# Reordering the start-up of a fused gated-attention and state-space kernel: where three turns' TensorE blocks stand

## The chip, the core and the metric

The kernel runs on one core of a Trainium2 chip. The metric is the device time of one execution in microseconds (us); of several runs the median counts. The engines are named as in the profile: PE is TensorE (PEld its weight loads), DVE is VectorE, ACT is ScalarE, POOL is GpSimd, SP is SyncE, which here only issues DMAs.

## What is computed

Four batches of eight heads, 768 steps, 48 features per head. A gated linear recurrence is followed by a projection, a second recurrence with a gate, and a projection back (float32 throughout; the weights arrive as float64):

```python
for t in range(S):
    state = alpha[:, :, t, :, None] * state + np.einsum('bhd,bhe->bhde', k[:, :, t], v[:, :, t])
    y[:, :, t] = np.einsum('bhd,bhde->bhe', q[:, :, t], state)
# x: y with the heads side by side, (4, 768, 384)
proj = x @ w_in                       # 384 -> 2 * 512
val, gate = proj[..., :512], proj[..., 512:]
for t in range(S):
    h = a[0, 0] * h + val[:, t, :]
    ys[:, t, :] = h
silu = gate * (1.0 / (1.0 + np.exp(-gate)))
return silu * ys @ w_out              # 512 -> 384
```

## The kernel before

**Tiling.** The 768 steps of a batch are cut into three groups of 256 steps, so there are N = 12 groups, each of two chunks of 128 steps (c = 0, 1). The recurrence is done by chunk: cumulative products of alpha (two DVE scans, one forwards, `prod`, one backwards, `inv`) scale the queries and keys into `Z`; `scores` multiplies them, `masks` keeps the causal part in `A`, `values` multiplies `A` with v, `keys` turns the keys into `ktm`, `state` sums keys times values, `carried` adds what the earlier chunks left. `join` copies the result out of PSUM into `y_sb` and puts the heads side by side in `xT` with eight small DMAs and two copies. Then four `block(n, cc)`, one for each 128 of the 512 inner features: `project` (12 PE matmul instructions, values first, then gate), `hidden` (a DVE scan of 256 steps), `gate` (Silu on ACT, and a product on POOL into `f`). `output(n)` multiplies `f` with w_out: 16 matmul instructions for two chunks, evacuated by ACT and stored by SP.

**Stages.** Everything is written out in program order, and every engine works its own part of that order strictly in turn; semaphores between the engines come from the tiles. So the order of the source lines is the order of each queue: if PE reaches a matmul whose input is not there, all later matmuls wait. In turn n of the last loop the projections of group n run beside the attention of group m = n + 1, the DVE steps of group n + 2 (the generator `products`, advanced by `go(count)`, `count` yields at a time) and the loads of group n + 3 (`ahead`).

Groups 0 to 2 are loaded with steps on the partitions (`load_natural`) and are turned by PE transposes (`turned`, L605; for keys and queries followed by a DVE product, `natural_qk`, L620). From group 3 on a layout is loaded (`load_raw`, four DMAs for each of a, k, q) that DVE can transpose itself (L660). For those groups `products` yields seven times: after turning a (with `first`, L671), after the scan `prod` (L674), after the scan `inv` (L695), after turning k, multiplying it (L704), turning q, multiplying it. `check_alpha` is a pass of ACT over the raw alphas (L631).

**Buffers that matter here.** Raw buffers: two sets, group m in set m % 2. v: two. `f`: one. `xT`, `Z`: two. PSUM banks 0, 1 and 6 go round for `mm`; pairs of banks (4, 5) and (2, 3) alternate for `pair_of`. Scans `hidden` wait in DVE's queue behind whatever stands before them.

**Lines to follow.** L1002 is the ACT copy of the turned alphas of group 2 into `aT`; L827 the matmuls of a block; L835 its scan, L842 its Silu, L843 its POOL product; L856 output matmuls; L864 and L865 their evacuation and store; L717 keys; L727 scores; L742 and L743 the far masks on ACT and POOL; L754 the near masks on DVE; L786, L765, L776 state, values, carried; L795, L796, L802 and L812 the join. L543 to L560 turn float64 words of the weights into float32, in the shadow of group 0's blocks; the last of these products, for w_out, is done on POOL at 44.4 us. L430 is `load_raw`, L445 `load_natural`, L454 `load_v`.

The functions that the diff touches:

Of the kernel before, what the change touches and what calls it, by code (L numbers as in the profile page):

```python
# [13 lines left out]
AF = mybir.ActivationFunctionType  # L14
# [337 lines left out]
def fast(  # L352
# [21 lines left out]
    nc = tc.nc  # L374
# [3 lines left out]
    C = 128  # L378
    G = 2
# [27 lines left out]
    def pair_of(*dims, dtype=FP32, which=None):  # L407
        if next(next_pair) if which is None else which:
            return [end_ps.tile([C, *dims], dtype, tag=f"b{b}", name="pair") for b in (4, 5)]
        t = both()  # L410
        n = dims[0] * dims[1]
        return [t[:, i, 0:n].rearrange("p (x y) -> p x y", x=dims[0]).bitcast(dtype) for i in range(2)]

    def both():
        return ps.tile([C, 2, 4 * C], FP32, tag="b23", name="pair")
# [5 lines left out]
    def load_raw(name, m, engines):  # L421


        b, g = divmod(m, NG)
        src = {"a": alpha, "q": q, "k": k}[name]
        t = raw_bufs[m % NR][name]
        n = 0
        for i in range(2):
            for odd in range(2):
                engines[n % len(engines)].dma_start(  # L430
                    out=t[ds(64 * i + 32 * odd, 32), :, 0:NT * D - 32 * odd],
                    in_=src[b, i::2, ds(g * GC, GC), :]
                    .rearrange("h (c j) d -> c h (j d)", c=32)[:, :, 32 * odd:])
                n += 1
# [3 lines left out]
    def natural(name, m):  # L438
        flat = raw_bufs[m % NR][name].rearrange("p h n -> p (h n)")[:, 0:G * H * 64]
        return flat.rearrange("p (c h d) -> p c h d", c=G, h=H)  # L440
# [10 lines left out]
    def load_v(m, engine, cs=range(G)):  # L451
        b, g = divmod(m, NG)
        for c in cs:
            engine.dma_start(out=vs[m % NV][:, c, :, 0:D],  # L454
                             in_=v[b, :, ds(g * GC + c * C, C), :].rearrange("h p d -> p h d"))
# [34 lines left out]
    alphas = aT[:, 0:4 * GC].rearrange("p (h n) -> p h n", h=4)  # L490
# [111 lines left out]
    def turned(name, m, c, tp):  # L602

        for p in range(4):
            nc.tensor.transpose(tp[:, p, :], natural(name, m)[:, c, 2 * p:2 * p + 2, :], ident)  # L605
# [17 lines left out]
    def check_alpha(m):  # L623

        if m < NAT:
            src = natural("a", m)[:, :, :, 0:D]
        else:
            src = raw_bufs[m % NR]["a"].rearrange("p h (j d) -> p h j d", d=D)[:, :, :, 0:32]
        _, x, y, z = src.shape
        junk = p1.tile([C, x, y, z], BF16, tag="junk", name="junk")  # L630
        nc.scalar.activation(junk, src, AF.Relu, bias=minus, accum_out=above[:, m:m + 1])  # L631
# [159 lines left out]
    def join(m, engines, later=False):  # L791

        y = ys.pop(m)
        y_sb = p2.tile([C, 4, GC], FP32, tag="y_sb", name="y_sb")
        nc.scalar.activation(y_sb[:, 1::2], y[1], AF.Copy)  # L795
        nc.scalar.activation(y_sb[:, 2], y[0][:, 1], AF.Copy)  # L796
        xT = xTs[m] = p2.tile([C, NK, GC], FP32, tag="xT", name="xT")

        def in_place():
            for h in (0, 4):  # L800
                kk, row = divmod(h * D, C)
                nc.scalar.activation(xT[ds(row, D), kk], y[0][ds(16 * h, D), 0], AF.Copy)  # L802

        if not later:
            in_place()
        for h in (1, 5, 3, 7, 2, 6):
            s, a = divmod(h, 4)
            d = 0
            while d < D:
                kk, row = divmod(h * D + d, C)  # L810
                size = min(D - d, C - row)
                engines[s].dma_start(out=xT[ds(row, size), kk], in_=y_sb[ds(64 * s + d, size), a])  # L812
                d += size
        return in_place
# [25 lines left out]
    def gate(n, cc, pg):  # L840
        sg = p2.tile([C, GC], FP32, tag="sg", name="sg")
        nc.scalar.activation(sg, pg, AF.Silu)  # L842
        return lambda: nc.gpsimd.tensor_mul(fs[n][:, cc, :], sg, hhs.pop((n, cc)))  # L843

    def block(n, cc):
        pv, pg = project(n, cc)
        hidden(n, cc, pv)
        gate(n, cc, pg)()

    def output(n, banks=(None, None)):  # L850
        b, g = divmod(n, NG)
        os = [mm(DM, b=b) for b in banks]

        def part(ccs, c):
            for cc in ccs:
                nc.tensor.matmul(os[c], fs[n][:, cc, ds(c * C, C)], w_out[:, cc, :],  # L856
                                 start=(cc == 0), stop=(cc == NI - 1))

        def finish():
            for c in range(G):  # L860
                part(range(split, NI), c)
            for c in range(G):
                o_sb = p3.tile([C, DM], FP32, tag="o_sb", name="o_sb")
                nc.scalar.activation(o_sb, os[c], AF.Copy)  # L864
                nc.sync.dma_start(out=out[b, ds(g * GC + c * C, C), :], in_=o_sb)  # L865

        split = NI - 1 if n else NI // 2
        for c in range(G):
            part(range(split), c)
        return finish  # L870


    SP, ACT = nc.sync, nc.scalar
# [98 lines left out]
    banks = pair_of(4, C, dtype=U32)  # L972
# [18 lines left out]
    for cc in range(NI):  # L991
# [4 lines left out]
            low_word(cc + 3)  # L996
        words(cc + 2)
        times()
    finish = output(0)
    for c, tp in enumerate(pair_of(4, C)):  # L1000
        turned("a", 2, c, tp)
        nc.scalar.activation(alphas[:, :, ds(c * C, C)], tp, AF.Copy)  # L1002
    check_alpha(2)
    load_raw("k", 3, [SP])
    load_raw("q", 3, [SP])
    for _ in products(2):
# [5 lines left out]
    for n in range(1, N):  # L1012
        m = n + 1
        att = m < N
        steps = products(n + 2) if n + 2 < N else iter(())

        def go(count):
            for _ in range(count):
                next(steps, None)


        def ahead():
            if n + 3 < N:
                loads(n + 3)
            if n + 2 < N:
                load_v(n + 2, SP)

        if n < 3:
            if n == 1:
                block(n, 0)  # L1030
                for times in [natural_qk(m, name, c, tp) for c in range(G)
                              for name, tp in zip("kq", pair_of(4, C))]:
                    times()
                block(n, 1)
            ahead()
            for c in range(G):
                keys(m, c)
            for c in range(G):
                scores(m, c)
            go(1)  # L1040
            for c in range(G):
                masks(m, c)
            if n == 2:
                block(n, 0)
                go(1)
                block(n, 1)
                go(1)
            else:
                block(n, 2)
                go(1)  # L1050
            state(m, 0)
            values(m, 0)
            values(m, 1)
            state(m, 1)
            carried(m, 0)
            carried(m, 1)
            join(m, (nc.gpsimd, nc.gpsimd) if m == 2 else (SP, SP))
            if n == 2:
                go(2)
                block(n, 2)  # L1060
            go(1)
            block(n, 3)
            go(10)
            output(n)()
            continue

        if n == 3:
            for c in range(G):  # L1070
                scores(m, c, 1 - c)
                masks_apart(m, c)
            for c in range(G):
                keys(m, c)
            ahead()
            go(4)
        else:
            state(n, 0)
            values(n, 0)
            values(n, 1)  # L1080
            state(n, 1)
            carried(n, 0)
            carried(n, 1)
            in_place = join(n, (SP, nc.gpsimd), later=True)
            if att:
                scores(m, 0, 1)
                masks_apart(m, 0)
                in_place()
                scores(m, 1, sc=[mm(4, C, b=b) for b in "01"])
                masks_apart(m, 1)  # L1090
                keys(m, 0, "6")
                keys(m, 1, "4")
            else:
                in_place()
            next_mm = itertools.cycle("160")
            ahead()
            go(4)
            output(n - 1, "50")()
        for cc in range(NI):
            block(n, cc)  # L1100
            go(1)
            if cc == 0 and n == N - 1:
                next(end, None)
            if cc == 2 and n > 3:
                for _ in itertools.islice(checks, 2):
                    pass
        if n == N - 2:
            end = check_end()
            next(end)
# [61 lines left out]
```

## Time and profile before

| | us |
|---|---|
| median of 3 runs (lowest, highest) | 291.07 (291.03, 291.84) |
| the profiled execution | 291.08 |
| its span, first to last instruction | 289.3 |
| busy: PE, PEld | 279.4, 227.2 |
| busy: DVE, POOL, ACT | 211.2, 139.2, 109.1 |
| DMA moved | 42.08 MB, mean 145 GB/s |

The granted TensorE clock is 1.000 over the whole span. The first 30 us are start-up: loads, turning and attention of groups 0 and 1. Group 0's blocks run from 30.25 us, its output from 40.72, turn one (n = 1) from 47.18, turn two's scores start at 72.19, turn three's at 93.90, and from there each turn takes 21.5 to 21.9 us. A row of the timeline gives start, duration, engine, line, operation, tiles and count; in brackets stands the idle time of the engine before it and what ended it. [...] neighbouring matmuls overlap; the distance from start to start is the time that one takes.

### The profile page before, as it was taken

The page shows a single profiled execution, that of the slowest core. Times are in us where ns is not written, and L with a number is a line of the kernel's source. Part 1 is how long each engine was busy: PE and PEld are TensorE (multiplying, and loading weights), DVE is VectorE, ACT ScalarE, POOL GpSimd, SP SyncE. Part 2 cuts the span into 40 slices and gives each one's busy share as a digit, 9 for nine tenths or more (in the row PEclk, how much of TensorE's full clock was granted, in tenths as well). Part 3 has the DMA queues.
Part 4 walks back from the last instruction along what each step waited for, and adds up shares of the span by engine and source line. Part 5 has one row for each costly group of instructions (what it writes and reads, how often), then busy time and mean ns, then how long its engine had stood idle before and what let it go on. Part 6 is the DMA issues. An engine that isn't in the chain of part 4 may idle for free. (4 is left out here: it accounts for less than half of the span.)

```text
span 289.3 us, 6236 instructions
## 1 busy us (share of the span) xinstructions
PE 279.4 (97%) x2353; PEld 227.2 (79%) x2353; DVE 211.2 (73%) x263; ACT 109.1 (38%) x242; POOL 139.2 (48%) x165
## 2 busy tenths in 40 slices
PE   7699999999999999999999999999999999999985
PEld 6478877885886988788788788788788788687874
DVE  5998896999999999399599599599589580131221
ACT  2447634432441626316316415416416415313110
POOL 7147792375532765526725725625734734633130
PEclk9999999999999999999999999999999999999999
DMA  9999969999997992992991991991892400201101
GB/s 130 163 162 299 376 129 185 173 250 211 231 220 106 221 200 53 215 205 54 228 189 43 217 204 42 206 212 48 191 198 77 113 2 25 73 0 30 69 5 61
DMA packets 70734, 42.08 MB, mean 145 GB/s; under 512 B 47508, under 2 KB 69656, under 8 KB 70696
## 3 DMA queue, kind: packets, MB, share of 16 engines
q1 hardware_dynamic: 68240, 39.78, 69.8%
q0 software_dynamic: 1408, 1.62, 2.3%
q8 instruction: 20, 0.33, 0.5%
q10 hardware_dynamic: 1048, 0.20, 0.4%
q14 instruction: 18, 0.15, 0.2%
HBM read 33.33 MB, written 4.72 MB: 131 GB/s over the span
## 5 line engine op out<-in xcount | busy, mean ns | idle before, releaser
L827 PE MATMUL mm<-xT,w_in 128*128 128x256 f32 x576 | 127.7, 380 | 0.3 <-ACT A L742 0.3
L827 PEld LDWEIGHTS mm<-xT,w_in 128*128 128x128 f32 x576 | 108.7, 190 | 17.7 <-issue 0.6
L843 POOL TENSOR_TENSOR f<-sg,hh 128x256 f32<-128x256 f32 x48 | 40.4, 843 | 87.2 <-ACT sg L842 61.8
L835 DVE TENSOR_TENSOR_SCAN hh<-a_dec,hh,mm 128x256 f32<-128x256 f32 x32 | 23.7, 741 | 49.6 <-PE mm L827 44.9
L856 PE MATMUL mm<-w_out,f 128*128 128x384 f32 x176 | 59.4, 489 | 0.1
L842 ACT ACTIVATE sg<-mm 128x256 f32<-128x256 f32 x48 | 18.5, 385 | 98.7 <-PE mm L827 96.6
L750 POOL TENSOR_TENSOR A<-A,mask 128x512 f32<-128x512 f32 x32 | 47.7, 1519 | 5.5 <-ACT A L749 5.4
L856 PEld LDWEIGHTS mm<-w_out,f 128*128 128x128 f32 x176 | 32.5, 190 | 21.4 <-POOL f L843 1.0
L812 POOL DMA_DIRECT2D xT<-y_sb x44 | 22.7, 521 | 28.4 <-ACT y_sb L796 26.8
L674 DVE TENSOR_TENSOR_SCAN prod<-aT,first 128x1024 f32<-128x1024 f32 x10 | 23.4, 2340 | 0.3
L695 DVE TENSOR_TENSOR_SCAN inv<-aT,last 128x1025 f32<-128x1025 f32 x10 | 22.9, 2294 | 0.3
L765 PE MATMUL pair<-A,v 128*64 128x128 f32 x352 | 21.3, 274 | 0.0
L864 ACT ACTIVATE o_sb<-mm 128x384 f32<-128x384 f32 x22 | 10.8, 491 | 25.4 <-PE mm L856 25.2
L727 PE MATMUL pair<-Z 48*128 48x128 f32 x272 | 18.9, 282 | 0.8 <-DVE first L640 0.3
L727 PEld LDWEIGHTS pair<-Z 48*128 48x128 f32 x272 | 16.4, 187 | 3.7 <-issue 2.1
L765 PEld LDWEIGHTS pair<-A,v 128*64 128x64 f32 x352 | 19.1, 137 | 0.0
L743 POOL TENSOR_TENSOR A<-A,mask 128x512 f32<-128x512 f32 x8 | 10.1, 1274 | 17.9 <-ACT A L742 17.9
L660 DVE STREAM_TRANSPOSE Z<-raw_k 128x1024 f32<-128x1024 f32 x9 | 18.4, 2047 | 0.0
L660 DVE STREAM_TRANSPOSE aT<-raw_a 128x1024 f32<-128x1024 f32 x9 | 18.4, 2046 | 0.0
L660 DVE STREAM_TRANSPOSE Z<-raw_q 128x1024 f32<-128x1024 f32 x9 | 18.2, 2024 | 0.0
L835 DVE TENSOR_TENSOR_SCAN hh<-a_dec,mm 128x256 f32<-128x256 f32 x16 | 10.8, 676 | 8.6 <-PE mm L827 7.0
L786 PEld LDWEIGHTS st<-v,ktm 128*64 128x64 f32 x320 | 11.4, 137 | 3.5 <-issue 3.5
(128 smaller groups left out, 300.7 us busy)
## 6 DMA issues: line engine op xcount, KB each, us to landing
raw_k<-in_k_dram SPq DMA_DIRECT2D x24, 192.0 KB, 5.3
raw_q<-in_q_dram SPq DMA_DIRECT2D x24, 192.0 KB, 6.6
v<-in_v_dram SPq DMA_DIRECT2D x24, 192.0 KB, 7.1
raw_a<-in_alpha_dram SPq DMA_DIRECT2D x23, 192.0 KB, 4.0
out_dram<-o_sb SPq DMA_DIRECT2D x22, 192.0 KB, 4.0
raw_a<-in_alpha_dram SPq DMA_DIRECT2D x18, 176.0 KB, 4.5
raw_k<-in_k_dram SPq DMA_DIRECT2D x18, 176.0 KB, 5.5
raw_q<-in_q_dram SPq DMA_DIRECT2D x18, 176.0 KB, 7.0
```

What stands on the lines that cost most here:

```text
L660: nc.vector.transpose(out=to.rearrange("p h (c j) -> p h j c", j=NT), in_=raw_bufs[m % NR][name].rearrange("p h (j d) -> p h j d", d=D)[:, ...
L674: nc.vector.tensor_tensor_scan(out=prod, data0=al, data1=first.rearrange("p h n -> p (h n)"), initial=0.0, op0=ALU.mult, op1=ALU.max)
L695: nc.vector.tensor_tensor_scan(out=inv[:, ::-1], data0=aT[:, ::-1], data1=lasts[:, 0:4 * GC + 1][:, ::-1], initial=0.0, op0=ALU.mult, op1= ...
L727: nc.tensor.matmul(sc[i][:, p, :], Z[rows, p, 1, cols], Z[rows, p, 0, cols], start=True, stop=True)
L750: nc.gpsimd.tensor_mul(A[:, i], A[:, i], mask_all())
L765: nc.tensor.matmul(ys[m][i][ds(64 * s, 64), e, ds(c * C, C)], v_sb[:, c, 2 * p + i, :], A[:, i, p, :], start=(c == 0 and e == 0), stop=Fal ...
L812: engines[s].dma_start(out=xT[ds(row, size), kk], in_=y_sb[ds(64 * s + d, size), a])
L827: nc.tensor.matmul(pj, w_in[cc][vg][:, kk, :], xT[:, kk, :], start=(kk == 0), stop=(kk == NK - 1))
L835: nc.vector.tensor_tensor_scan(out=hh, data0=a_dec[:, cc:cc + 1].to_broadcast([C, GC]), data1=pv, initial=prev_h[cc][:, GC - 1:GC] if n % ...
L842: nc.scalar.activation(sg, pg, AF.Silu)
L843: return lambda: nc.gpsimd.tensor_mul(fs[n][:, cc, :], sg, hhs.pop((n, cc)))
L856: nc.tensor.matmul(os[c], fs[n][:, cc, ds(c * C, C)], w_out[:, cc, :], start=(cc == 0), stop=(cc == NI - 1))
```

## The change

Four edits, all of order:

- `output` takes a function `between`, called after chunk 0's first-half matmuls and before chunk 1's. For group 0 it turns group 2's alphas, copies them and checks them; before, this came after both chunks' first half.
- Turn one starts with the turning of group 2's keys and queries and has its blocks 0 and 1 together behind it; a step of `products` stands between the two. The next group's loads are split: alphas before group 2's keys, and keys, queries and v behind the join.
- Turn two starts with the loads and block 0, then keys and scores; its block 2 comes before the state and not after the join. Group 2's join issues half of its DMAs from SP and half from POOL, not all from POOL.
- Turn three takes two steps of `products` ahead of its blocks and not four, and what is left of them after its last block.

```diff
-    def output(n, banks=(None, None)):
+    def output(n, banks=(None, None), between=lambda: None):
...
         split = NI - 1 if n else NI // 2
-        for c in range(G):
-            part(range(split), c)
+        part(range(split), 0)
+        between()
+        part(range(split), 1)
         return finish
...
-    finish = output(0)
-    for c, tp in enumerate(pair_of(4, C)):
-        turned("a", 2, c, tp)
-        nc.scalar.activation(alphas[:, :, ds(c * C, C)], tp, AF.Copy)
-    check_alpha(2)
+
+    def alphas_2():
+        for c, tp in enumerate(pair_of(4, C)):
+            turned("a", 2, c, tp)
+            nc.scalar.activation(alphas[:, :, ds(c * C, C)], tp, AF.Copy)
+        check_alpha(2)
+
+    finish = output(0, between=alphas_2)
...
             if n == 1:
-                block(n, 0)
                 for times in [natural_qk(m, name, c, tp) for c in range(G)
                               for name, tp in zip("kq", pair_of(4, C))]:
                     times()
+                block(n, 0)
+                go(1)
                 block(n, 1)
-            ahead()
+                load_raw("a", n + 3, [SP])
+            else:
+                ahead()
+                block(n, 0)
             for c in range(G):
                 keys(m, c)
...
             if n == 2:
-                block(n, 0)
-                go(1)
                 block(n, 1)
                 go(1)
-            else:
-                block(n, 2)
-                go(1)
+            block(n, 2)
+            go(1)
             state(m, 0)
...
-            join(m, (nc.gpsimd, nc.gpsimd) if m == 2 else (SP, SP))
-            if n == 2:
-                go(2)
-                block(n, 2)
+            join(m, (SP, nc.gpsimd) if m == 2 else (SP, SP))
+            if n == 1:
+                for name in "kq":
+                    load_raw(name, n + 3, [SP])
+                load_v(n + 2, SP)
             go(1)
             block(n, 3)
...
             for c in range(G):
                 keys(m, c)
             ahead()
-            go(4)
+            go(2)
...
+        go(10)
         if n == N - 2:
```

## Prediction

> **What bounds the kernel now.** I read the page's busy shares first, then TensorE's timeline from end to end, then the waits of the one stretch in which it was not periodic, and last the landing times of the loads that this stretch uses.
>
> ```profile
> PE 279.4 (97%) x2353; PEld 227.2 (79%) x2353; DVE 211.2 (73%) x263; ACT 109.1 (38%) x242; POOL 139.2 (48%) x165
> ```
>
> TensorE is busy 97% of the span. Only 10 us are idle, so the change can gain little by shortening another engine; it gains or loses by what it does to TensorE's waits. A busy share hides waits inside a group, so I take the time from one group's start to the next one's. TensorE's timeline (start, busy, line, operation, count):
>
> ```profile
> 40.72 3.11 PE L856 MATMUL mm<-w_out,f 128*128 128x384 f32 x8
> 43.66 1.04 PE L605 MATMUL pair<-ident,raw_a 128*128 128x128 f32 x8
> ...
> 47.18 2.75 PE L827 MATMUL mm<-xT,w_in 128*128 128x256 f32 x12
> 49.77 0.60 PE L605 MATMUL pair<-ident,raw_k 128*128 128x128 f32 x4
> ...
> 51.52 2.76 PE L827 MATMUL mm<-xT,w_in 128*128 128x256 f32 x12
> ...
> 65.49 5.54 PE L856 MATMUL mm<-w_out,f 128*128 128x384 f32 x16
> 70.87 1.04 PE L717 MATMUL mm<-ident,Z 128*128 128x128 f32 x8
> 72.19 2.06 PE L727 MATMUL pair<-Z 48*128 48x128 f32 x32 [0.28 <-DVE Z L704]
> 74.55 5.49 PE L827 MATMUL mm<-xT,w_in 128*128 128x256 f32 x24 [0.31 <-ACT A L742]
> 79.97 0.67 PE L786 MATMUL st<-v,ktm 128*64 128x48 f32 x16
> ...
> 93.90 2.06 PE L727 MATMUL pair<-Z 48*128 48x128 f32 x32
> 95.89 1.09 PE L717 MATMUL mm<-ident,Z 128*128 128x128 f32 x8
> 96.82 10.53 PE L827 MATMUL mm<-xT,w_in 128*128 128x256 f32 x48
> ```
>
> From 96.82 to 280 us the groups repeat with the same lengths and no wait; nothing in the change touches their number. Their lengths are my unit prices: a block of 12 matmuls 2.61 us (48 in 10.46, from 96.82 to 107.27), an output of 16 in 5.18 (113.59 to 118.77), scores 1.99, four transposes 0.44. Set against these, the second turn waits: output 65.49 to 70.87 is 5.38, so 0.20 lost; keys and scores 70.87 to 74.55 are 3.68 against 1.99 + 0.93 = 2.92 (93.90 to 96.82), so 0.76 lost; two blocks 74.55 to 79.97 are 5.42 against 5.28, so 0.14. **1.10 us in all.** The weight loads of that stretch name who ended the waits:
>
> ```profile
> 69.47 0.94 PEld L856 LDWEIGHTS mm<-w_out,f 128*128 128x128 f32 x4 [0.57 <-POOL f L843]
> ...
> 72.16 1.89 PEld L727 LDWEIGHTS pair<-Z 48*128 48x128 f32 x32 [0.49 <-PE mm L717]
> 74.52 0.73 PEld L827 LDWEIGHTS mm<-xT,w_in 128*128 128x128 f32 x4 [0.47 <-ACT A L742]
> ```
>
> The first waits for the last gate of block (1,3), which POOL can only start at 67.90 because eight join DMAs stood ahead of it. The second needs the third chunk's Z for queries, which DVE finishes at 72.04. The third is labelled ACT, but that copy was long under way: the sequencer's own wait ended at 74.46, with the landing of an xT DMA issued from POOL.
>
> ```profile
> L812 POOL DMA_DIRECT2D xT<-y_sb x8: 497/507/566, 63.8 to 67.4; - x8
> ...
> DMA to landing us min/median/max: 6.9/7.9/8.1
> ```
>
> This is the answer on tile xT: eight issues of 0.5 us each, but 6.9 to 8.1 us to land, so the last is there at 75.4.
>
> [...] POOL's small xT pieces took 7.9 us behind SP's key and query loads. [...] of the second query load's 16 increments the fifteenth comes at 48.37 and the last at 50.74 us. [...] in the window 45.5 to 48 us one packet of queue 8 took 3.7% of 16 engines' 2.5 us, 1.48 us, and one of queue 14 2.2%, 0.88 us; together 2.36 us[...].
>
> **The change, part by part.**
>
> *Alphas inside the first output half.* No instruction is added. Now eight output matmuls run 40.72 to 43.66 (in them 0.35 us of wait for w_out's second block, which stays, because it falls within chunk 0) and the eight transposes follow. After it, chunk 0's output ends at about 42.37, the alphas of chunk 0 run to 42.81 (their load landed at 42.2), and those of chunk 1 must wait for their load: issued 39.5, to landing at most 3.9, so 43.40. From a release to the first matmul pass 0.15 to 0.2 us (at L856: released 41.58, matmul 41.72), so they start at 43.6. TensorE had 0.88 + 1.30 us to do up to 43.40 before; now 0.6 to 0.8 us is idle. I take **+0.74**. The second half then starts near 45.3, past its last gate (45.09), and ends at 47.92 instead of 47.18. DVE's scans start 0.7 us earlier (44.9 for 45.56).
>
> *Keys and queries of the third group ahead of block (1,0).* Sixteen transposes, 1.75 us, change places with a block of 2.59 us. The block was the cover of the query load. The answer on tile raw_q for 40 to 53 us:
>
> ```profile
> L445 SPq DMA_DIRECT2D raw_q<-in_q_dram x2: 1095/1116/1137, 41.8 to 43.0; - x2
> ...
> DMA to landing us min/median/max: 5.2/6.5/7.7
> ```
>
> Issued at 41.79 and 43.02, they land at 46.99 and 50.74. Before, the four transposes that need the second run at 51.08, with 0.3 us to spare. After, keys 0, queries 0 and keys 1 run 47.92 to 49.23, and then TensorE waits to 50.74 + 0.16 = 50.90: **+1.67**. Behind it stand all later matmuls; block (1,0), whose inputs are ready, can't pass. If the load came by 49.1 it would cost 0. SP's queue up to it is unchanged, [...] so I take the full price. Its multiply on DVE is not late: the inverse scan ends near 50.3, and its four multiplies near 52.7.
>
> *Order on DVE.* Turn a of group 3 comes one block sooner, at about 54.0 when its load has landed (issued 46.3, +7.6); it needs nothing else. TensorE now stands 2.4 us later at equal work, so masks (60.8), Z keys (69.1) and Z queries (72.3) of group 3 meet scores that start at 76.6, not 72.19: the 0.39 + 0.37 waits go. The next late thing is xT.
>
> *Join.* Half of the eight xT issues move from POOL to SP, ahead of key, query and value loads that stood before them. y_sb comes at about 66.2 (TensorE's carried ends 65.2, then copies of 0.60 and 0.38). Four issues at 0.6 end at 68.6, and behind only the four alpha loads (landed by 67.1) they need 2 to 2.7 us as on an idle queue: 71. POOL's half: 4 x 0.5 from 66.2, the same. Block (2,0), now straight after output(1), starts at 73.1. So the xT wait goes, with 2 us to spare. POOL's gate (1,3) is ready at 69.3, and its use is at 71.8: the 0.20 goes. All **-1.10**. One pair of blocks becomes two single ones; single ones cost 2.59 to 2.79, so **+0.05**.
>
> *Loads moved.* SP's keys, queries, values for later turns stand behind the join and leave at 68.5 instead of 62.3. The engines catch up at 0.85 us a load: values of group 3 land at about 79 (use at 83.9), the last query load for group 5 at 90.6. The first DMA after a pair of value loads was held until about then each time (85.47 to 89.17 for join(3)), so join(3) lands by 97, and block (3,0) starts at 98.1: hidden, with 1 us. The single alpha load for group 4 keeps its place.
>
> *go(2) and go(10) in turn three.* The inverse scan and later steps move between the four hidden scans. Adding up DVE's rows (scan 2.29, turn 2.05, multiply 1.2, hidden 0.7) from 94.0, the last Z multiply ends near 111.7; scores (5) start at 112.4. Now it ends at 105.9. So 5 us of slack become 0.6, at no cost. DVE waited 4.28 us at 120.34, which takes the lag up.
>
> **Sum.** 0.74 + 1.67 - 1.10 + 0.05 = +1.36. The profiled execution took 291.08 us (span 289.3, 1.8 around it), the median is 291.07: **292.4 us**.
>
> **Rivals.** *The query load lands earlier.* [...] the second wait goes and the change is 291.08 + 0.74 - 1.10 + 0.05 = 290.8. [...] Against: the same load order and nearly the same instruction count. The sign turns at a landing of 49.4. Chance with all landings between (290.4 to 291.9): 0.25. *Neither load makes TensorE wait*, because chunk 1's alphas land too: 290.0, faster. Against: that load has 16 even increments at 43.26 to 43.40. 0.10. *DVE becomes the bound:* if it runs over 0.6 us late in turn three, scores (5) wait; a scan took 2.80 instead of 2.29 once, a multiply 2.25 instead of 1.2, both beside POOL. Two such cost 1 us: 293.3. 0.10. The forecast as summed, 291.9 to 292.9: 0.55.
>
> **Numbers.** What can be told from no change is 0.3%, 0.87 us: 290.2 to 291.9. Faster holds the third case and a little of the second, 0.12; same 0.25; slower 0.63. The range leaves out the 290.0 case and the far end of the last: 290.4 to 293.3.
>
> **What would show it.** A gap before the last four L605 query transposes, ended by raw_q; one of 0.7 before the second alphas; no gap at L727 and L827 from 70 to 80; scores (4) start near 95.2. No gap at the queries, or scores (4) before 94, proves me wrong.

## The result and the profile after

The changed kernel takes **294.14 us** (median of 4 runs, 293.93 to 294.93) beside 291.38 for the kernel before in the same session: ratio 1.0094, interval 1.0072 to 1.0117. It is slower by 0.9%. Ratios here are taken over the runs within 1.5% of a kernel's fastest, so for kernels with a wide spread they can differ a little from the quotient of the medians. The profiled execution took 294.01 us, span 292.3, so **+2.93** against the 291.08 of the profile before.

The page's busy line: DVE has 3.3 us more work in the same number of instructions, TensorE's is unchanged, so the time went into waits.

```profile
PE 279.3 (96%) x2353; PEld 226.7 (78%) x2353; DVE 214.5 (73%) x263; ACT 109.4 (37%) x242; POOL 140.9 (48%) x161
```

TensorE's timeline of the start (start, busy, line, operation, count; in brackets the idle time before and its releaser):

```profile
40.40 1.82 PE L856 MATMUL mm<-w_out,f 128*128 128x384 f32 x4
43.24 0.63 PE L605 MATMUL pair<-ident,raw_a 128*128 128x128 f32 x4 [1.02 <-DMA raw_a<-in_alpha_dram]
44.44 0.63 PE L605 MATMUL pair<-ident,raw_a 128*128 128x128 f32 x4 [0.57 <-DMA raw_a<-in_alpha_dram]
44.90 4.04 PE L856 MATMUL mm<-w_out,f 128*128 128x384 f32 x12
...
51.47 0.63 PE L605 MATMUL pair<-ident,raw_q 128*128 128x128 f32 x4 [1.22 <-DMA raw_q<-in_q_dram]
51.93 5.34 PE L827 MATMUL mm<-xT,w_in 128*128 128x256 f32 x24
```

Three waits for loads, where one of 0.7 and one of 1.67 had been forecast: chunk 0's alphas wait too. Before, TensorE had left the turning at 51.52 with block (1,0) done; now the block stands behind the last wait of 1.22 us and does not fill it, and TensorE leaves at 51.93 with the block (2.59) still to do: 0.41 + 2.59 = **+3.00**. The same engine later:

```profile
68.50 5.32 PE L856 MATMUL mm<-w_out,f 128*128 128x384 f32 x16
73.66 2.75 PE L827 MATMUL mm<-xT,w_in 128*128 128x256 f32 x12
76.25 1.04 PE L717 MATMUL mm<-ident,Z 128*128 128x128 f32 x8
77.21 2.06 PE L727 MATMUL pair<-Z 48*128 48x128 f32 x32
79.20 5.45 PE L827 MATMUL mm<-xT,w_in 128*128 128x256 f32 x24
...
95.92 2.06 PE L727 MATMUL pair<-Z 48*128 48x128 f32 x32
97.91 1.09 PE L717 MATMUL mm<-ident,Z 128*128 128x128 f32 x8
98.83 6.64 PE L827 MATMUL mm<-xT,w_in 128*128 128x256 f32 x30
105.76 4.15 PE L827 MATMUL mm<-xT,w_in 128*128 128x256 f32 x18 [0.28 <-DVE hh L835]
```

No bracket from 68 to 96: the waits of turn two are gone. The stretch from the first block of turn one to scores (4) took 42.38 us without block (1,0) before, and takes 95.92 - 51.93 - 2.59 = 41.40 now: **-0.98**. But the four blocks of turn three are torn apart at 105.76; they take 98.83 to 109.84 = 11.01 us where they took 10.46: **+0.55**. The weight loads in front of them say for how long and for whom:

```profile
105.76 3.75 PEld L827 LDWEIGHTS mm<-xT,w_in 128*128 128x128 f32 x18 [0.69 <-DVE hh L835]
```

From 109.84 all periods are the old ones. The rest of the difference stands at the very end. DVE's last copy, first before (span 289.35), then after (span 292.28):

```profile
286.46 0.30 DVE L1139 COPY_PREDICATED end<-good,o 128x128 f32<-128x128 uint8 x1 [0.45 <-PE o L1135]
```

```profile
288.79 0.30 DVE L1146 COPY_PREDICATED end<-good,o 128x128 f32<-128x128 uint8 x1 [0.45 <-PE o L1142]
```

From its end to the end of the span are 3.19 us, before 2.59. **+0.60**; a shorter wait for the flag ahead of the last output (1.13 us for 1.37 at its weight loads) gives back 0.24. In all 3.00 - 0.98 + 0.55 + 0.60 - 0.24 = 2.93, for this pair of profiles.

### The profile page after: what moved, and what is told of

Its sections match the earlier page's. It is cut to its first block, busy times and chain, and to the rows that moved or that the text cites. A ratio compares the mean times of both kernels' runs of the same rounds, so it can differ in the third digit from the quotient of the medians.

```text
span 292.3 us, 6230 instructions
## 1 busy us (share of the span) xinstructions
PE 279.3 (96%) x2353; PEld 226.7 (78%) x2353; DVE 214.5 (73%) x263; ACT 109.4 (37%) x242; POOL 140.9 (48%) x161
## 5 line engine op out<-in xcount | busy, mean ns | idle before, releaser
L750 POOL TENSOR_TENSOR A<-A,mask 128x512 f32<-128x512 f32 x32 | 51.7, 1644 | 5.7 <-ACT A L749 5.5
L812 POOL DMA_DIRECT2D xT<-y_sb x40 | 20.7, 522 | 29.9 <-ACT y_sb L796 26.8
L695 DVE TENSOR_TENSOR_SCAN inv<-aT,last 128x1025 f32<-128x1025 f32 x10 | 25.7, 2570 | 0.3
L743 POOL TENSOR_TENSOR A<-A,mask 128x512 f32<-128x512 f32 x8 | 10.1, 1270 | 13.1 <-ACT A L742 13.1
```

The costliest lines, as they stand in the source:

```text
L695: nc.vector.tensor_tensor_scan(out=inv[:, ::-1], data0=aT[:, ::-1], data1=lasts[:, 0:4 * GC + 1][:, ::-1], initial=0.0, op0=ALU.mult, op1= ...
L750: nc.gpsimd.tensor_mul(A[:, i], A[:, i], mask_all())
```

## The experiments

### The start: are the landing times of group 2's loads the cause?

*Control (before_again): the kernel before, once more.*

> The kernel before, once more, for a second profile of its start. Ratio 1.000 on every theory. If the landing of the second query load is set by what stands in the DMA queues, it comes at 50.7 us again, give or take 0.7 (51.33 in the changed kernel's profile); if the changed order itself made it later, at 50.7 within 0.2. In the first case the alpha loads, too, move by up to 1 us between profiles without any change in time, because nothing waits for them here.

291.19 us (14 runs), ratio 0.9997 (0.9986 to 1.0008). What its profile tells is the spread of landings in an unchanged kernel: second query load at 51.23 us (50.74 in the first profile), alphas at 42.80 and 43.97 (42.20 and 43.40). TensorE lost only some 0.3 us by it, at the last query transposes (51.37 for 51.08): the block in front of the turning covers the rest.

*One edit undone each.* Block (1,0) ahead of the turning again (q_back):

```diff
             if n == 1:
+                block(n, 0)
                 for times in [natural_qk(m, name, c, tp) ...]:
                     times()
-                block(n, 0)
                 go(1)
```

> The changed kernel with block (1,0) back ahead of the turning of group 2's keys and queries. Theory A (the landing of the second query load sets the time of the start): the block of 2.59 us again covers the 1.38 us of wait, so 1.4 us less than the changed kernel, 292.7, and no idle time at the query transposes. Theory B (the changed order on DVE is what costs, TensorE would have waited elsewhere): within 0.3 of the changed kernel, 294.1.

292.81 us (6 runs), ratio 1.0060 (1.0036 to 1.0084): 1.33 under the changed kernel, as theory A had it. Its profile has no wait at the turning. And the alphas behind both halves again (alphas_back):

```diff
-    finish = output(0, between=alphas_2)
+    finish = output(0)
+    alphas_2()
```

> The changed kernel with the third group's alphas turned after both chunks' first output half again. Theory A: TensorE reaches the query transposes sooner but leaves them when the load lands, so the wait there grows by what the alpha waits (1.94 us in the profile) lose; time within 0.3 of the changed kernel, 294.1. The working of the prediction, which added the two waits: 0.7 to 1.9 us less, 292.2 to 293.4.

The profiled execution took 294.14 us, as theory A had it: the waits don't add up. TensorE reaches the keys' transposes 1.3 us sooner (47.47 for 48.78), but leaves the turning when the query load lands (51.80 for 51.93); the wait at the queries is now 2.33 us in one piece. But the median is 296.28 (5 runs; ratio 1.0172, 1.0151 to 1.0194), worse than with the edit, which neither theory had. The other four runs, 295.66 to 297.12, have a mean granted TensorE clock of 0.994 instead of 0.999.

*Each edit alone in the kernel before.* First the alphas' (alphas_only):

```diff
-    finish = output(0)
     ...
+    finish = output(0, between=alphas_2)
```

> The kernel before the change with its first start edit alone: the third group's alphas turned between the two halves of the first output. Theory A (the wait is set by when the alpha loads land, 43.3 to 44.4 for chunk 1 in the profiles seen so far, against 42.85 when TensorE asks for it): a wait of 0.5 to 1.9 us in all before the second half, none of it taken up later because the query load that follows is covered by block (1,0): 291.9 to 293.0. Theory B (TensorE's lateness is absorbed by the waits of turn two, which are for DVE and POOL and don't move with it): scores (4) where they were and 291.2 to 291.6.

292.20 us (22 runs), ratio 1.0036 (1.0021 to 1.0052): +0.76 in the medians, theory A. But not all of the lateness lasts: in its profile turn one is 1.24 us late (first block at 48.42 for 47.18), and from output (2) on (89.48 for 88.65) it is 0.83, since the wait for xT before block (2,0) has taken up 0.41. Three of the 22 runs, 294.09 to 294.54, have a clock of 0.994; none of them was profiled. And the queries' edit alone (queries_only):

```diff
             if n == 1:
-                block(n, 0)
                 for times in [natural_qk(m, name, c, tp) ...]:
                     times()
+                block(n, 0)
                 block(n, 1)
```

> The kernel before the change with its second start edit alone: keys and queries of the third group turned ahead of block (1,0), the block behind them. TensorE asks for the last query load near 48.5; in the profiles so far that load landed between 48.4 and 51.3. Theory A (the landing sets the cost): a wait of 0 to 2.9 us by execution, 1.7 to 2.5 in most, some executions with a granted clock of 0.994 instead of 1.0; the median 292.6 to 294.5, a wide spread. Theory B (the block hides nothing, since waits for DVE in turn one take up the lateness): 291.2 to 291.8.

294.94 us (292.32 to 295.81, 7 runs), ratio 1.0096 (1.0061 to 1.0131). Theory A, with its spread. The three runs with a clock of 1.0 took 292.32, 293.32 and 293.46; the four with 0.994 took 294.94 to 295.81. This time the profiled execution was one of the latter. Its timeline at the turning:

```profile
48.81 0.60 PE L605 MATMUL pair<-ident,raw_k 128*128 128x128 f32 x4
51.71 0.63 PE L605 MATMUL pair<-ident,raw_q 128*128 128x128 f32 x4 [2.30 <-DMA raw_q<-in_q_dram]
52.18 7.03 PE L827 MATMUL mm<-xT,w_in 128*128 128x256 f32 x24
```

and the busy table by windows (window, its length, then busy time and count of each engine; behind POOL's stand the granted clock, the DMA share and GB/s):

```profile
50.00:51.70 1.70, 0.00 (x0) 0.02 (x1) 1.64 (x1) 0.00 (x0) 0.00 (x0) 1.00 1.10 205
51.70:52.70 1.00, 0.99 (x6) 0.91 (x7) 0.96 (x2) 0.00 (x0) 0.00 (x0) 0.81 1.36 176
52.70:53.70 1.00, 1.00 (x3) 0.78 (x3) 1.00 (x3) 0.00 (x0) 0.00 (x0) 0.50 1.46 166
...
54.70:55.70 1.00, 1.00 (x4) 0.82 (x3) 0.75 (x1) 0.00 (x0) 0.00 (x0) 0.50 0.40 69
55.70:56.70 1.00, 1.00 (x6) 0.87 (x6) 0.00 (x0) 0.00 (x0) 0.00 (x0) 0.98 1.09 307
```

After the wait TensorE runs at half its clock for some 3.4 us (an estimate from the granted shares of 0.81, 0.50 and 0.98 in these windows); two blocks take 52.18 to 59.05 = 6.87 us instead of 5.18, so the wait costs a further **1.69 us**. That is 0.6% of the span, the missing 0.006 of the mean clock. A wait of this length did not bring it each time: alphas_back's profile has 2.33 us, the full clock behind it and a mean of 0.999. What decides it was not shown.

*The loads earlier (loads_ahead).* In the changed kernel, group 2's six loads ahead of the second group's xT DMAs on SP:

```diff
-    join(1, (SP, SP))
     for name in "akq":
         pair(name, 2, SP, SP)
+    join(1, (SP, SP))
     load_raw("a", 3, [SP])
```

> The changed kernel, with the six loads of the third group's alphas, keys and queries issued on SP ahead of the eight xT DMAs of the second group instead of behind them. The rest is as in the changed kernel. Theory A (the landing time of these loads is what makes TensorE wait at the start): they land some 4 us earlier, the waits of 1.02 and 0.57 us before the two halves of the alphas and of 1.22 us before the last query transposes go, xT lands by 47 and is not needed before 49, scores (4) start near 93.4 instead of 95.92, and the time falls by 2.3 to 2.8 us, to 291.2 to 291.8. Theory B (the waits come from something else that stands in front of these transposes, the raw buffers or the order on TensorE): the loads cannot leave earlier or the waits stay, 293.8 to 294.4.

292.02 us (19 runs), ratio 1.0018 (1.0007 to 1.0029), 2.1 us under the changed kernel. The alphas land at 39.47 and 40.49, the second query load at 44.97. TensorE's timeline:

```profile
42.15 1.04 PE L605 MATMUL pair<-ident,raw_a 128*128 128x128 f32 x8
43.02 4.09 PE L856 MATMUL mm<-w_out,f 128*128 128x384 f32 x12
...
48.26 0.60 PE L605 MATMUL pair<-ident,raw_q 128*128 128x128 f32 x4
48.70 4.05 PE L827 MATMUL mm<-xT,w_in 128*128 128x256 f32 x18
53.04 1.13 PE L827 MATMUL mm<-xT,w_in 128*128 128x256 f32 x4 [0.29 <-DVE hh L835]
```

All three waits for loads are gone, xT is in time: the landing is the cause. The time is 0.2 above theory A's range; a small wait for DVE has come up behind them (0.70 us at its weight loads), since the four multiplies of the turned keys and queries now stand ahead of hidden scan (1,0).

*Early or late.* The prediction set an instruction packet of queue 8 and one of queue 14, together 2.36 us, beside the 2.37 us by which the last increment of the second query load came late; the traces bear on this. Fourteen of the sixteen profiles have these loads in the old order. In seven of them (before, before_again, alphas_only, queries_only, after, alphas_back, both_back) a 16 KiB instruction packet of DMA queue 8 starts at 44.9 to 46.9 us and takes 1.05 to 1.46; there the last of the load's 16 increments comes 1.66 to 2.38 us behind the fifteenth, and the load lands at 50.0 to 51.6. In the other seven this packet came at 36.4 to 39.5 already; there the last increment lags by 0.41 at most, and the load lands at 48.4 to 50.2. Queue 14's packet stands at 46.9 to 48.6 in all fourteen. Queue 8's packet and the lag go together in all fourteen, but no run moved the packet alone, and why it comes early or late is open.

### Turn one: what does the moved DVE step do?

*Both start edits undone, turns two and three as changed (both_back).*

> The changed kernel with both edits of the start undone; turn two, its join and turn three stay changed. Theory A: no wait at alphas or queries, the 1.0 us that turn two gained stays, turn three keeps its wait of 0.55 on DVE: 0.4 to 0.5 us under the kernel before, 290.9 where that is 291.4. Theory B: within 0.5 of the changed kernel. If turn two's edits gain nothing by themselves (TensorE was merely late): 291.9.

292.88 us (6 runs), ratio 1.0058 (1.0040 to 1.0077). All three expectations fell: with no start wait left, the gain of turn two should have made it faster than before. DVE in turn one, before the change:

```profile
53.93 0.74 DVE L835 TENSOR_TENSOR_SCAN hh<-a_dec,hh,mm 128x256 f32<-128x256 f32 x1
54.58 2.04 DVE L660 STREAM_TRANSPOSE aT<-raw_a 128x1024 f32<-128x1024 f32 x1
...
56.99 1.29 DVE L754 TENSOR_TENSOR A<-pair,mask 128x512 f32<-128x512 f32 x2
```

and in both_back:

```profile
53.99 2.05 DVE L660 STREAM_TRANSPOSE aT<-raw_a 128x1024 f32<-128x1024 f32 x1
...
56.29 0.74 DVE L835 TENSOR_TENSOR_SCAN hh<-a_dec,hh,mm 128x256 f32<-128x256 f32 x1
...
56.95 2.27 DVE L674 TENSOR_TENSOR_SCAN prod<-aT,first 128x1024 f32<-128x1024 f32 x1
59.13 1.26 DVE L754 TENSOR_TENSOR A<-pair,mask 128x512 f32<-128x512 f32 x2
```

Turn a of group 3 stands ahead of hidden scan (1,1), and the product scan ahead of the masks. POOL's product for (1,1) then starts at 57.17 instead of 54.88 (in the next kernel below, with the old order), POOL's far masks behind it at 59.70 instead of 57.08, and TensorE waits for a scan and for masks (its weight loads):

```profile
57.08 2.46 PEld L827 LDWEIGHTS mm<-xT,w_in 128*128 128x128 f32 x12 [0.44 <-DVE hh L835]
...
61.01 0.85 PEld L765 LDWEIGHTS pair<-A,v 128*64 128x64 f32 x16 [0.26 <-POOL A L743]
62.28 0.42 PEld L765 LDWEIGHTS pair<-A,v 128*64 128x64 f32 x8 [0.42 <-POOL A L743]
```

In the changed kernel TensorE is nearly 3 us later at this place (keys at 57.11 for 54.25), and its profile shows none of these waits. So, the same kernel without that step between the blocks (both_back_turn_one):

```diff
-                go(1)
                 block(n, 1)
                 load_raw("a", n + 3, [SP])
```

> The kernel with both start edits undone (292.88 before), and on DVE turn a of group 3 behind the scores again instead of between blocks (1,0) and (1,1), so that in turn one hidden scan (1,1) stands ahead of turn a and the masks ahead of the product scan, as in the kernel before the change. Theory A (turn one's DVE order costs 0.94 us in the profile, and more in executions whose load for group 3 lands later): values (2) take 1.86 instead of 2.50, block (1,2) does not wait, and the time falls by 0.9 to 1.7, to 291.2 to 292.0, of which 0.55 is turn three's wait. Theory B (turn one's order is not the cause, the moved loads or the join are): 292.7 to 292.9.

291.57 us (22 runs), ratio 1.0006 (0.9997 to 1.0014): 1.31 less, theory A. DVE's order is the old one, and these waits are gone. This run also settles turn two: TensorE leaves the turning at 51.56, as early as before the change, and has scores (4) at 92.96, so the stretch is 41.40 us as in the changed kernel. The 0.98 us are the edits' and not the lateness's.

### Turn three: why do the blocks wait for a hidden scan?

DVE in the changed kernel:

```profile
75.22 0.75 DVE L835 TENSOR_TENSOR_SCAN hh<-a_dec,hh,mm 128x256 f32<-128x256 f32 x1 [2.52 <-PE mm L827]
...
100.33 0.69 DVE L835 TENSOR_TENSOR_SCAN hh<-a_dec,mm 128x256 f32<-128x256 f32 x1 [0.87 <-PE mm L827]
100.94 0.84 DVE L681 TENSOR_TENSOR ratio<-prod,last 128x4 f32<-128x4 f32 x1
...
102.02 3.10 DVE L695 TENSOR_TENSOR_SCAN inv<-aT,last 128x1025 f32<-128x1025 f32 x1
105.05 0.66 DVE L835 TENSOR_TENSOR_SCAN hh<-a_dec,mm 128x256 f32<-128x256 f32 x1
```

DVE idles 2.52 us for block (2,0), which now stands ahead of group 4's steps; and later a scan of 3.10 us stands between two hidden scans. Before the change it took 2.29 us and began ahead of POOL's mask multiplies; now it begins beside them. Before:

```profile
94.84 2.29 DVE L695 TENSOR_TENSOR_SCAN inv<-aT,last 128x1025 f32<-128x1025 f32 x1
95.77 7.11 POOL L750 TENSOR_TENSOR A<-A,mask 128x512 f32<-128x512 f32 x4 [5.38 <-ACT A L749]
```

In the changed kernel:

```profile
97.79 8.40 POOL L750 TENSOR_TENSOR A<-A,mask 128x512 f32<-128x512 f32 x4 [5.55 <-ACT A L749]
```

First I filled the idle stretch (turn_early):

```diff
                 ahead()
+                go(1)
                 block(n, 0)
```

> The changed kernel, with turn a of group 4 issued on DVE ahead of block (2,0) instead of after the scores, so that it fills the 2.52 us at 72.7 to 75.2 in which DVE waits for that block; each later step of that group moves up by one place. Theory A (turn three's wait of 0.55 us comes from where the inverse scan stands, between the first two hidden scans of block three, and from its 3.10 us beside POOL's masks): the inverse scan stays between them, hidden scan (3,1) is no earlier, the wait stays and the time is 293.9 to 294.3. Theory B (DVE is simply 2 to 2.5 us late because of that idle stretch): the wait goes, scores (5) start 0.55 us sooner at 113.1, and the time is 293.5.

294.41 us (6 runs), ratio 1.0116 (1.0093 to 1.0139): theory B fell, the wait stays (at 103.65; the blocks take 10.91 us). The profiled execution alone took 292.07: in it the second query load landed at 48.38 and TensorE didn't wait for it. The other five took 293.98 to 295.55, two of them at a clock of 0.994. Then the inverse scan ahead of block (3,0) as well (go_three_turn_early):

```diff
             ahead()
-            go(2)
+            go(3)
```

> As the one before, and in turn three a third step of group 5, the inverse scan, stands ahead of block (3,0) instead of behind its hidden scan. Theory A (place of the inverse scan): with DVE some 2 us earlier the scan runs 97.7 to 100, hidden scan (3,0) starts near 100.3 as in the changed kernel, hidden scan (3,1) near 103 instead of 105.05, the PEld wait of 0.69 us at 105.76 goes, blocks three take 10.46 instead of 11.01 and the time is 293.4 to 293.6. Theory B (something else, for example the xT or gate of that block, makes block three wait): 294.1.

294.47 us (6 runs, one of them at a clock of 0.994), ratio 1.0104 (1.0079 to 1.0129): my theory A fell too. The scan ran earlier, at 98.35, but again 3.11 us long behind a ratio of 1.06, and the wait moved one block ahead, to 102.09; the blocks take 11.04 us. In both cases POOL was at its mask multiplies when the scan began. The next two kernels start from the one of the next section (290.94): POOL's multiplies for group 4 left out (no_masks_three), and the old four steps restored (go_four_again).

```diff
             nc.scalar.activation(A[:, i], sc[i], AF.Copy)
-            nc.gpsimd.tensor_mul(A[:, i], A[:, i], mask_all())
+            if m != 4:
+                nc.gpsimd.tensor_mul(A[:, i], A[:, i], mask_all())
```

> The kernel of four_more_dmas (290.94), and in turn three POOL's four multiplies by the causal mask are left out for group 4 only, so that group's scores stay unmasked. Theory A (the inverse scan of group 5 is 3.10 us instead of 2.29, and the ratio in front of it 0.83 instead of 0.17[...]): the ratio takes 0.17, the scan 2.29, hidden scan (3,1) starts 1.4 us sooner, blocks three take 10.46 instead of 11.01 and the time falls by 0.5 to 0.6, to 290.3 to 290.5. Theory B (the scan is slower for another reason, or the wait comes from its place between hidden scans alone): scan 2.8 to 3.1, or the wait stays, 290.8 to 291.1.

```profile
99.05 0.14 DVE L681 TENSOR_TENSOR ratio<-prod,last 128x4 f32<-128x4 f32 x1
99.22 0.18 DVE L687 RECIPROCAL last<-prod 128x4 f32<-128x4 f32 x1
99.43 2.29 DVE L695 TENSOR_TENSOR_SCAN inv<-aT,last 128x1025 f32<-128x1025 f32 x1
101.64 0.66 DVE L836 TENSOR_TENSOR_SCAN hh<-a_dec,mm 128x256 f32<-128x256 f32 x1
```

Ratio and scan have their usual lengths (0.83 and 3.10 in four_more_dmas) and the wait for DVE is gone, as theory A had it. The gain that it forecast did not show: 290.79 us (22 runs), ratio 0.9986 (0.9977 to 0.9996), not told from the 0.9987 of four_more_dmas, where theory A had 0.5 less. The blocks take 10.73 us, because in this profile another wait of 0.41 us, at the issue of a weight load, has come in; whether that is so in each run is open. So the 0.55 us of turn three are read off profiles and not shown by a time. How POOL's masks lengthen DVE's steps was not shown, only which steps: beside them the inverse scan and the ratio grow (2.29 to 3.10, 0.17 to 0.84); two hidden scans don't (0.69 and 0.66 in the changed kernel and in no_masks_three alike), nor does a transpose (2.02 in go_four_again, at 102.06, and 2.03 in no_masks_three). POOL's four masks take 8.40 us, against 5.09 in turn_early, where DVE stands idle for 2.2 us beside them.

```diff
             ahead()
-            go(2)
+            go(4)
```

> The kernel of four_more_dmas (290.94), with four steps of group 5 ahead of block (3,0) again, as before the change, instead of two. Theory A (DVE comes to turn three some 3 us later against TensorE than before the change, so the steps don't fit ahead of the block any more; two steps are the lesser evil): hidden scan (3,0) starts near 103 instead of 97.78, block (3,1)'s gate waits 3 us for it, and the time rises by 2 to 3 us, to 293 to 294. Theory B (it is the move from four steps to two that costs the 0.55 us): the wait goes and the time falls to 290.3 to 290.5.

296.34 us (6 runs), ratio 1.0172 (1.0147 to 1.0196): theory A in its direction, but 5.4 us more and not 2 to 3.

```profile
104.60 7.55 PEld L827 LDWEIGHTS mm<-xT,w_in 128*128 128x128 f32 x29 [3.87 <-DVE hh L835]
```

One wait of 3.87 us, and behind it again half the clock (0.53 and 0.62 in the two stretches of 2 us from 104 on); all six runs have a clock of 0.994 or less. So with the other edits in place the step from four to two is no fault: DVE turns group 5's alphas 1.15 us ahead of scores (4) in the changed kernel (94.77 and 95.92), and 4.2 us ahead of them in the control (90.27 and 94.47). By these times it is that lateness that brings the scan beside the masks; no run took it away whole.

### The end: why 0.6 us more behind the last copy?

The stretch is 3.18 or 3.19 us in all eight profiles of kernels with the changed join up to here, and 2.59 to 2.77 in the four of kernels with the old one. SP issues four DMAs more, so the last output counts on another of eight semaphores (counters that in the traces take 16 increments from each landing). SP waits for these at the end one after the other: the last output's is the seventh before the change and the third in the changed kernel. With five more to look at, the last output lands at 290.65 in the changed kernel and SP's closing waits are through at 291.37; in both_back_turn_one 287.69 and 288.41. With one more, the two times are 288.32 and 288.42 before the change, 288.66 and 288.77 in before_again. In the test four more DMAs, late, bring the count round (four_more_dmas):

```diff
-                nc.sync.dma_start(out=out[b, ds(g * GC + c * C, C), :], in_=o_sb)
+                for at in ((0, DM // 2) if n in (8, 9) else (0,)):
+                    cols = ds(at, DM // 2 if n in (8, 9) else DM)
+                    nc.sync.dma_start(out=out[b, ds(g * GC + c * C, C), cols], in_=o_sb[:, cols])
```

> The kernel with both start edits undone and turn one's DVE order restored (291.57 before), in which the output of groups 8 and 9 leaves in four more DMAs: each o_sb goes out as two halves of its columns. Nothing waits for them. Theory A (the last 0.4 us of every kernel with the changed join come from SP's closing waits: the last output DMA counts on the third of eight semaphores, and five more waits of 0.06 to 0.4 us follow its landing, where before it counted on the last but one): with four more DMAs the last output counts on the same semaphore as before the change, the stretch from the last copy on DVE to the end is 2.6 to 2.75 us instead of 3.15, and the time falls by 0.3 to 0.5 us, to 291.1 to 291.3. Theory B (the tail is longer for another reason): 291.5 to 291.7, tail unchanged.

290.94 us (22 runs), ratio **0.9987** (0.9977 to 0.9996), 0.63 less than without. DVE's last copy and the span, first of both_back_turn_one, then of four_more_dmas:

```profile
core 0 of [0], span 289.3 us
...
285.85 0.30 DVE L1146 COPY_PREDICATED end<-good,o 128x128 f32<-128x128 uint8 x1 [0.45 <-PE o L1142]
```

```profile
core 0 of [0], span 289.1 us
...
286.19 0.30 DVE L1148 COPY_PREDICATED end<-good,o 128x128 f32<-128x128 uint8 x1 [0.45 <-PE o L1144]
```

The copy ends 0.34 later and the span 0.26 earlier (289.06 for 289.32): the tail is 2.57 for 3.18. This kernel is a little faster than before the change, by 0.13%: it has the changed turns two and three, without the start edits and without the step between turn one's blocks. The changed kernel with its causes mended in place (loads ahead, turn one's DVE order, four more DMAs; mended):

> The changed kernel with both of its start edits kept, and three things mended: the third group's loads leave ahead of the second group's xT (as in loads_ahead, 292.02), turn a of group 3 stands behind the scores on DVE (as in both_back_turn_one), and the outputs of groups 8 and 9 leave in four more DMAs. If the three causes add up: 0.6 us for the wait of block (1,1) at 52.4 and the values' wait in turn one, 0.4 for the tail, so 290.7 to 291.2, and faster than before by 0.1 to 0.2%. If they don't: 291.6 to 292.0.

291.20 us (14 runs), ratio 0.9990 (0.9978 to 1.0001), not told from the kernel before; the causes add up at the edge of the range. The three repairs take 2.9 us off the changed kernel. Against loads_ahead it is 0.82 less, 0.6 of it the tail; turn one's wait at 53.03 stayed, since its cause is the multiplies ahead of hidden scan (1,0), not the step that I moved.

## Why the prediction was wrong, point by point

| step | forecast | changed kernel's profile |
|---|---|---|
| alphas and queries at the start | +0.74 + 1.67 | +3.00 |
| turn two, with one more single block | -1.10 + 0.05 | -0.98 |
| loads moved | 0 | 0 |
| turn three's DVE order | 0 | +0.55 |
| the end | 0 | +0.60 - 0.24 |
| sum | +1.36 | +2.93 |

The miss of 1.57 is 0.59 at the start, 0.07 in turn two, 0.55 in turn three and 0.36 at the end.

**The start** was right in mechanism: both edits put TensorE ahead of loads that had been covered, and loads_ahead shows it. The signs that it named came: gaps ahead of the second alphas and of the last query transposes, none at scores and blocks from 70 to 80, scores (4) at 95.92 for 95.2. The size failed at "Issued at 41.79 and 43.02, they land at 46.99 and 50.74": one execution's landing, taken as the kernel's. Over the 14 profiles with that order of loads it is 48.38 to 51.58 us, in the two of the unchanged kernel 50.74 and 51.23, in the changed one 51.33, issued 0.87 later. That is 0.59 us of the miss. The same holds for chunk 0's alphas, forecast free because "their load landed at 42.2": they landed at 43.11. This costs nothing more, since 0.74 and 1.67 are not two prices: the second was worked out from a TensorE that the first had made late, and their sum is one wait for the query load, as alphas_back's profile shows. Alone the alphas cost 0.76, and that 0.74 was forecast is in part luck: the profile has 1.24, of which turn two takes up 0.41. The queries alone cost 0.9 to 2.0 at full clock. The rival of an early landing is real, and the reason given against it is not: with "the same load order and nearly the same instruction count" the instruction packet was out of the way in seven of 14 profiles. It came in turn_early's profile, at 48.38 and 292.07 us. What no case held is the half clock behind a long wait, another 1.69 us in queries_only's profile. The changed kernel's own four runs are at 0.997 to 1.0; turn_early and go_three_turn_early, with the same start, had 0.994 in three of twelve.

**Turn two** was right in size, and the waits go without TensorE's lateness too (both_back_turn_one). Right also is that xT lands ahead of block (2,0) (70.5 for 71). Join (3)'s last piece landed at 99.3 and not by 97, with no visible wait.

**Turn three** failed at "So 5 us of slack become 0.6, at no cost". I looked at the last step of the chain, the queries' multiply before scores (5), which was in time. The step that was late is a hidden scan in the middle, behind an inverse scan that takes 3.10 us beside POOL's masks (2.29 in no_masks_three, without them). The rival "DVE becomes the bound" had the operations right (a scan longer beside POOL) and the place wrong: not scores (5), but a block. (Its 293.3 should be 293.4: 292.44 plus 1.)

**Turn one's** moved step was waved through with "it needs nothing else": true of its inputs, but hidden scan (1,1), POOL's far masks and the masks stand behind it. In the changed kernel TensorE is late enough to cover it; without the start edits it costs 1.31 us. So the forecast of nothing came true by luck.

**The end** was not looked at, though the join's four DMAs from POOL to SP were in the list. The longer tail is the join's (four_more_dmas, 0.63); in the second profile of the unchanged kernel it is 2.77 us and not 2.59, so 0.4 to 0.6 of the difference. The 0.24 given back has no such cause: over the profiles that wait is 1.05 to 1.65.

## What to carry to other kernels

A block that stands ahead of a late load is its cover: before it is moved, take the load's landing as a range over several executions, since one profile's 0.3 us of spare time may be none in the next (50.74 and 51.23 us in two profiles of the same kernel here). For each step moved on a queue, list what stands behind it there, not only what it needs; and look at what the other engine does beside a long scan: the inverse one took 3.10 us beside POOL's mask multiplies and 2.29 without them (what that is worth was seen here in profiles only). A wait of TensorE can cost more than its length: the one of 2.30 us in queries_only's profile cost 1.69 us more, by the half clock behind it. That two short waits are safe is not shown.

## What the runs showed of the hardware

- A single TensorE wait inside dense work was followed by about 3.4 us at half the clock in two profiles, after 2.30 us (queries_only: a granted clock of 0.50 from 52.70 to 55.70, 1.69 us more for 24 matmuls) and 3.47 us (go_four_again: 0.53 and 0.62 in two stretches of 2 us); after 2.33 us in alphas_back's profile it was not, nor after the three of 1.02, 0.57 and 1.22 us in the changed kernel's.
- The landing of one load differed by 3.2 us over 14 profiles (48.38 to 51.58, issued at 42.95 to 44.84). Its last of 16 increments lags the fifteenth by 1.66 to 2.38 us in the seven with an instruction packet of queue 8 at 44.9 to 46.9, and by 0.02 to 0.41 in the seven without.
- A DVE scan of 1025 elements took 3.10 us beside POOL's mask multiplies and 2.29 with these left out; the ratio of 4 elements in front of it 0.83 and 0.14.
- Four DMAs more on SP took 0.6 us off the stretch behind the last copy (3.18 us in both_back_turn_one, 2.57 in four_more_dmas). SP's closing waits lasted 0.72 us past the last landing with five semaphores still to look at (after, both_back_turn_one), and 0.10 and 0.11 with one (before, before_again).
